# Sketch attention and a cosine router on one core: expert logits taken from the query product, four ticks per half, bfloat16 rank compares

## Chip, cores and metric

One core of one Trainium2 chip runs the whole program. The metric is device time in microseconds (us), the median of several executions; shorter is better.

## What is computed

Attention over 16 heads (batch 4, heads 4, sequence 1088, head size 32) with a polynomial feature map, then a router that sends each of 4352 tokens to one of 8 experts:

```python
a, b = S1 @ x, S2 @ x;  phi = outer(a, b)          # 8 x 8 = 64 features of q and of k
kv = sum_s phi(k)[s] v[s];  z = sum_s phi(k)[s]
x = (phi(q) @ kv) / (phi(q) @ z + 1e-6)             # heads side by side: 4352 x 128
xn = x / (|x| + 1e-6);  en = emb / (|emb| + 1e-6)
logits = xn @ en.T / tau;  e = argmax(logits)
out[token] = softmax(logits)[e] * (relu(x @ w1[e]) @ w2[e])
```

All data is float32.

## The kernel before

**Halves, tiles, groups.** The batch is worked in two halves m = 0, 1 (two batches each, 2176 tokens). A half has 17 tiles of 128 tokens, taken in the five groups of `GROUPS`: four of 4 tiles and a last one of 1 tile. Per group there are two helpers, `keys` (L296) and `queries` (L345), each a list of small functions:

- `keys`: `tr` transposes the tiles on TensorE (L267) and ScalarE copies them out (L269); `ab` forms both sketches (L280); `b` copies the second one (ScalarE, L286); `prod` multiplies them into 64 features (VectorE, L291, `kp`); `kv` adds the products with V into the PSUM bank `acc` (L327). After the last tile VectorE copies `acc` into `kz` (L335, L336).
- `queries`: `tr`, `ab`, `b`, `prod` as above (`qp`); `tr_qp` transposes the features (L372) and ScalarE copies them (L375, `qpT`); `nd` multiplies by `kz` (L383: 33 columns per head, value and denominator) and VectorE divides (L389 to L391, `xg`); `xt` transposes the result again (L397, copied by L399) and `logit` multiplies it by the normed experts `enT` (L412, copied by L415); `best` takes the maximum (L419); `squares` gives the norms (L404).
- `router`, every 8 tiles (`SPAN`): `pick` makes one-hot rows and counts (L452 to L462), `place` finds each token's slot (L471 to L482), `mark` compares 128 lane numbers with each token's rank (L487, `row`, one float32 operand), `store` finishes the norm (one GpSimd power, L493, and two VectorE operations), `write` stores `xg` to DRAM.

**Tables.** `plan_early` and `plan_late` turn counts into a list of 10 and of 31 expert blocks; `table` compares block keys with the slots (L541), multiplies by token digits (L545) and sums through TensorE (L550), one load of `row[:, t]` and one product per tile. The result lists which tokens each block gathers.

**Blocks.** 41 blocks of 128 tokens: `fetch` gathers rows (GpSimd, L605), `turn` transposes them (L611), `weights` copies an expert's weights (L623, L626 or L628), `up` is the first product (L637), `down` the second (L652), and GpSimd scatters the result (L657).

**What sets the order.** The order is written by hand: each function is put at a tick and a rank, and the program emits tick after tick, by rank within one. In the kernel before a group starts every second tick, and its steps spread over the ticks behind:

```python
put(0, 60, tr); put(1, 51, ab); put(1, 61, b); put(1, 63, prod); put(5 if late else 3, 30, kv)   # keys
put(0, 61, tr); put(1, 50, ab); put(1, 60, b); put(1, 62, prod)                                  # queries
put(3, 10, tr_qp); put(4, 20, nd); put(5, 20, xt); put(5, 80, squares); put(6, 10, logit); put(6, 70, best)
```

The keys of half 0 take ticks 0 to 9, the keys of half 1 with the queries of half 0 ticks 10 to 19, the queries of half 1 ticks 20 to 29, and the blocks start at tick 31. Each engine works in its own order and waits where an input is late. PSUM: two buffers `ps_t` for small results, two `ps_big`, and one bank each for `acc` and `ab`.

Of the kernel before, what the change touches and what calls it, by code (L numbers as in the profile page):

```python
# [13 lines left out]
I32 = mybir.dt.int32  # L14
# [19 lines left out]
GROUPS = ((0, 4), (4, 8), (8, 12), (12, 16), (16, 17))  # L34
SPAN = 8
ROW = DM + E + 1
DEN_EPS = 1e-6
# [16 lines left out]
def kernel(  # L54
# [47 lines left out]
    v_sb = [consts.tile([P, H + 1, NC, D], F32, name=f"v{m}") for m in range(NM)]  # L102
# [9 lines left out]
    def load_v(m, i):  # L112
        nc.sync.dma_start(
            v_sb[m][:, :H, i * NK:(i + 1) * NK].rearrange("p h c d -> p h (c d)"),
            bass.AP(tensor=v.tensor, offset=v.offset + (2 * m + i) * H * S * D,
                    ap=[[NK * D, P], [S * D, H], [1, NK * D]]))

    def load_rest(m):
        for i in range(2):
            r = slice(i * HALF, (i + 1) * HALF)  # L120
            at = (2 * m + i) * H * S * D + SK * D
            for t, src in ((k_rest[m][r], k), (v_sb[m][r, :H, NC - 1], v)):
                nc.sync.dma_start(t, bass.AP(tensor=src.tensor, offset=src.offset + at,
                                             ap=[[D, HALF], [S * D, H], [1, D]]))

    k_sb, q_sb = [None] * NM, [None] * NM
    emb_sb = consts.tile([E, DM], F32, name="emb_sb")
    tau_sb = consts.tile([E, 1], F32, name="tau_sb")
    for m in range(NM):
        k_sb[m] = rows_p.tile([P, H, 2, NK, D], F32, tag="rows", name=f"k{m}")  # L130
        for i in range(2):
            load_k(m, i)
            load_v(m, i)
        load_rest(m)
        q_sb[m] = rows_p.tile([P, H, NC, D], F32, tag="rows", name=f"q{m}")
        load_q(m)
        if m == 0:
            nc.sync.dma_start(emb_sb[:], emb)
            nc.sync.dma_start(tau_sb[:], bass.AP(tensor=tau.tensor, offset=tau.offset, ap=[[0, E], [1, 1]]))
# [9 lines left out]
    for m in range(NM):  # L149
        nc.gpsimd.memset(v_sb[m][:, H], 1.0)  # L150
# [38 lines left out]
    nc.gpsimd.memset(half_c, 0.5)  # L189

    rows = [tc.dram_tile([n, ROW], F32, name=f"rows{n}") for n in (2 * S, N)]

    def iota(shape, pattern, base, mult, name):
        ti = work.tile(shape, I32, tag="iota", name=name + "_i")
# [15 lines left out]
    lane_b = consts.tile([P, P], BF16, name="lane_b")  # L210
    nc.vector.tensor_copy(lane_b, lane)
    tok_i = consts.tile([P, 3, NT], I32, name="tok_i")
    nc.gpsimd.iota(tok_i[:, 0].rearrange("p (m c) -> p m c", m=NM), pattern=[[2 * S, NM], [1, NC]], base=1,
# [3 lines left out]
    digits = consts.tile([P, 2, NT], F32, name="digits")  # L217
# [6 lines left out]
    for w in (2, SPAN + 1):  # L224
# [11 lines left out]
    enT = consts.tile([P, E], F32, name="enT")  # L236
    kz = [consts.tile([P, 2, 2, 2, D + 1], F32, name=f"kz{m}") for m in range(NM)]
# [3 lines left out]
    def prep_emb():  # L241
        sq = work.tile([E, DM], F32, tag="emb", name="emb_sq")
# [53 lines left out]
    def keys(m, c0, c1, put, late):  # L296
# [6 lines left out]
        def ab(ps):  # L303
            s["ab"] = sketch(ps[:, 256:], s["kT"], n)
# [7 lines left out]
        def kv():  # L312
# [3 lines left out]

            end = ps_small()[:, :4 * D].rearrange("p (a n) -> p a n", a=2) if c1 == NC else None
            for c in range(c0, c1):
                rest = c == NC - 1
                for i in range(2) if rest else (c // NK,):  # L320
                    r = slice(i * HALF, (i + 1) * HALF) if rest else slice(0, P)
                    for p in range(2):
                        for u in range(2):
                            h = 2 * p + u
                            vo = v_sb[m][r, h, c]
                            own = acc[m][:, i] if not rest or i == 0 else end
                            nc.tensor.matmul(  # L327
                                own[u * HALF:(u + 1) * HALF, p], s["kp"][r, c - c0, h],
                                bass.AP(tensor=vo.tensor, offset=vo.offset,
                                        ap=[list(vo.ap[0]), [(H - h) * NC * D, 2], [1, D]]),  # L330
                                start=p == 0 and (c == 0 or own is end), stop=rest, skip_group_check=True)
            if c1 == NC:
                for u in range(2):
                    r = slice(u * HALF, (u + 1) * HALF)
                    nc.vector.tensor_copy(kz[m][r, :, :, u], acc[m][r, :, :, :D + 1])  # L335
                    nc.vector.tensor_add(kz[m][r, 1, :, u], kz[m][r, 1, :, u], end[r, :, :D + 1])  # L336
# [6 lines left out]
    xg, ssq = {}, {}  # L343

    def queries(m, c0, c1, put):  # L345
# [3 lines left out]
        g = (m, c0 // SPAN)  # L349
        at = c0 % SPAN  # L350
        own = slice(at, at + n)

        def tr():
            if at == 0:
                xg[g] = work.tile([P, SPAN, ROW], F32, tag="xg", bufs=3, name="xg")
                ssq[g] = work.tile([P, SPAN], F32, tag="ssq", name="ssq")
            s["qT"] = turned(None if n == 1 else q_sb[m][:, :, c0:c0 + 4], q_rest[m], n, "qT")

        def ab(ps):
            s["ab"] = sketch(ps[:, :256], s["qT"], n)  # L360
# [7 lines left out]
        def tr_qp():  # L368
            ps = ps_big()
# [4 lines left out]
            s["qpT"] = work.tile([P, 2, 512], F32, tag="qpT", name="qpT")  # L374
            nc.scalar.copy(s["qpT"][:, :, :w], ps[:, :, :w])  # L375

        def nd():
            ps = ps_big().rearrange("p b (u n) -> p (b u) n", u=2)
# [8 lines left out]
            hs = ps[:, :n, :2 * W].rearrange("p n (h d) -> p n h d", h=H)  # L387
            rc = work.tile([P, 4, H], F32, tag="rc", name="rc")
            nc.vector.tensor_scalar_add(rc[:, :n], hs[:, :, :, D], DEN_EPS)  # L389
            nc.vector.reciprocal(rc[:, :n], rc[:, :n])  # L390
            nc.vector.tensor_mul(xg[g][:, own, :DM].rearrange("p n (h d) -> p n h d", h=H), hs[:, :, :, :D],  # L391
                                 bview(rc[:, :n], [[H, n], [1, H], [0, D]]))

        def xt():
            ps = ps_small()
            for j in range(n):
                nc.tensor.transpose(ps[:, j * P:(j + 1) * P], xg[g][:, at + j, :DM], ident)  # L397
            s["xT"] = work.tile([P, 512], F32, tag="xT", name="xT")
            nc.scalar.copy(s["xT"][:, :w], ps[:, :w])  # L399

        def squares():
            for j in range(n):
                sq = work.tile([P, DM], F32, tag="sq", name="sq")
# [3 lines left out]
        def logit():  # L407
            ps = ps_small()[:, :4 * E].rearrange("p (n e) -> p n e", n=4)
            for j in range(n):
                for u in range(2):  # L410
                    r = slice(u * HALF, (u + 1) * HALF)
                    nc.tensor.matmul(ps[r, j], s["xT"][:, j * P + u * HALF:j * P + (u + 1) * HALF], enT,  # L412
                                     start=True, stop=True)
            s["lg"] = work.tile([P, 4, E], F32, tag="lg", name="lg")
            nc.scalar.copy(s["lg"][:, :n], ps[:, :n])  # L415

# [341 lines left out]
```

## Time and profile before

| what | us |
|---|---|
| time, median of 3 runs (283.9 to 286.25) | 285.73 |
| the profiled execution's own time | 285.32 |
| its span, first to last instruction | 283.5 |
| TensorE (PE) busy in it | 237.2 (84%) |
| VectorE (DVE) busy | 139.4 (49%) |
| ScalarE (ACT) busy | 117.9 (42%) |
| GpSimd (POOL) busy | 101.2 (36%) |

The profile is one execution. A matrix product in float32 stands in it as two records. A window row gives, for one stretch, the busy time of each engine and the granted TensorE clock as a share of 2.4 GHz (0.50 is 1.2 GHz). A timeline row gives start, length, engine, line, operation, tiles, count, and in brackets how long the engine stood idle before it and what ended that wait.

### The profile page before, as it was taken

The page shows a single profiled execution, that of the slowest core. Times are in us where ns is not written, and L with a number is a line of the kernel's source. Part 1 is how long each engine was busy: PE and PEld are TensorE (multiplying, and loading weights), DVE is VectorE, ACT ScalarE, POOL GpSimd, SP SyncE. Part 2 cuts the span into 40 slices and gives each one's busy share as a digit, 9 for nine tenths or more (in the row PEclk, how much of TensorE's full clock was granted, in tenths as well). Part 3 has the DMA queues.
Part 4 walks back from the last instruction along what each step waited for, and adds up shares of the span by engine and source line. Part 5 has one row for each costly group of instructions (what it writes and reads, how often), then busy time and mean ns, then how long its engine had stood idle before and what let it go on. Part 6 is the DMA issues. An engine that isn't in the chain of part 4 may idle for free. (4 is left out here: it accounts for less than half of the span.)

```text
span 283.5 us, 6567 instructions
## 1 busy us (share of the span) xinstructions
PE 237.2 (84%) x2558; PEld 226.7 (80%) x2558; DVE 139.4 (49%) x444; ACT 117.9 (42%) x315; POOL 101.2 (36%) x105
## 2 busy tenths in 40 slices
PE   1897788695939398597799999999999999999950
PEld 1786678694929288497799999999999999999950
DVE  6331445666872562437863455555544444444500
ACT  2222346435233344544564444444444444444420
POOL 4000000202000620715326765556666655554230
PEclk9995999959595856979999999999999999999995
DMA  5999999640300210111001211111011111121000
GB/s 197 258 314 205 318 341 338 190 161 16 145 20 2 86 46 0 48 64 48 19 21 34 48 41 30 41 33 41 27 35 38 39 38 34 33 37 30 18 0 0
DMA packets 22062, 24.32 MB, mean 86 GB/s; under 512 B 5321, under 2 KB 18004, under 8 KB 22032
## 3 DMA queue, kind: packets, MB, share of 16 engines
q1 hardware_dynamic: 19408, 18.79, 22.8%
q0 software_dynamic: 2624, 5.11, 7.0%
q8 instruction: 20, 0.33, 0.5%
q14 instruction: 10, 0.08, 0.1%
HBM read 18.09 MB, written 6.26 MB: 86 GB/s over the span
## 5 line engine op out<-in xcount | busy, mean ns | idle before, releaser
L637 PE MATMUL ps_big<-xTb,w1b 128*128 128x128 f32 x656 | 82.7, 281 | 1.9 <-DVE gate L645 1.9
L637 PEld LDWEIGHTS ps_big<-xTb,w1b 128*128 128x128 f32 x656 | 78.6, 196 | 2.6 <-DVE w1b L623 1.6
L638 ACT ACTIVATE hT<-ps_big 128x1024 f32<-128x1024 f32 x41 | 42.0, 1025 | 67.3 <-PE ps_big L637 67.2
L657 POOL DMA_INDIRECT out_dram<-y,dst_i x41 | 42.0, 1024 | 62.8 <-ACT y L654 59.5
L605 POOL DMA_INDIRECT xs<-rows,src_i x41 | 47.9, 1168 | 12.6 <-PE ps_t L611 7.8
L613 DVE COPY xTb<-ps_t 128x128 f32<-128x128 f32 x41 | 11.9, 291 | 59.8 <-PE ps_t L611 59.8
L652 PE MATMUL ps_acc<-w2b,hT 128*128 128x128 f32 x336 | 41.0, 275 | 0.0
L652 PE MATMUL ps_ab<-w2b,hT 128*128 128x128 f32 x320 | 40.0, 280 | 0.0
L652 PEld LDWEIGHTS ps_acc<-w2b,hT 128*128 128x128 f32 x336 | 39.2, 192 | 0.0
L652 PEld LDWEIGHTS ps_ab<-w2b,hT 128*128 128x128 f32 x320 | 38.5, 197 | 0.0
L493 POOL TENSOR_TENSOR xg<-ssq,half_c 128x8 f32<-128x8 f32 (+1 forms) x6 | 7.8, 1300 | 80.6 <-ACT lg L415 80.6
L623 DVE COPY w1b<-w_sb 128x1024 f32 x41 | 28.5, 696 | 9.0 <-issue 8.0
L628 DVE COPY w2b<-w_sb 128x1024 f32 x31 | 21.6, 698 | 0.0
L291 DVE TENSOR_TENSOR qp<-ps_ab,qb 128x1024 f32<-128x1024 f32 (+1 forms) x10 | 10.6, 1062 | 20.3 <-ACT kb L286 16.4
L611 PE MATMUL ps_t<-ident,xs 128*128 128x128 f32 x41 | 11.7, 285 | 4.9 <-DMA xs<-rows,src_i 4.9
L291 DVE TENSOR_TENSOR kp<-ps_ab,kb 128x1024 f32<-128x1024 f32 (+1 forms) x10 | 10.6, 1060 | 9.1 <-ACT kb L286 9.1
L383 PE MATMUL ps_big<-kz,qpT 128*64 128x66 f32 x272 | 14.7, 270 | 0.0
L375 ACT COPY qpT<-ps_big 128x1024 f32<-128x1024 f32 (+1 forms) x10 | 8.8, 885 | 12.6 <-PE ps_big L372 12.6
L383 PEld LDWEIGHTS ps_big<-kz,qpT 128*64 128x64 f32 x272 | 13.5, 178 | 0.0
L327 PE MATMUL ps_acc<-v,kp 128*64 128x64 f32 (+1 forms) x272 | 12.3, 255 | 1.2 <-DVE kz L336 1.2
L327 PEld LDWEIGHTS ps_acc<-v,kp 128*64 128x64 f32 (+1 forms) x272 | 10.8, 164 | 3.1 <-issue 2.6
L397 PE MATMUL ps_t<-ident,xg 128*128 128x128 f32 x34 | 7.2, 341 | 7.3 <-DVE mx L419 4.5
(162 smaller groups left out, 282.8 us busy)
## 6 DMA issues: line engine op xcount, KB each, us to landing
w_sb<-in_moe_w_dram SPq DMA_DIRECT2D x16, 512.0 KB, 7.9
rows<-xg SPq DMA_DIRECT2D x6, 548.0 KB, 2.9
q<-in_q_dram SPq DMA_DIRECT2D x4, 544.0 KB, 8.0
k<-in_k_dram SPq DMA_DIRECT2D x4, 512.0 KB, 5.8
v<-in_v_dram SPq DMA_DIRECT2D x4, 512.0 KB, 7.1
xs<-rows,src_i POOLq DMA_INDIRECT x41, 2.8
out_dram<-y,dst_i POOLq DMA_INDIRECT x41, 2.3
rows<-xg SPq DMA_DIRECT2D x3, 68.5 KB, 1.6
```

Source lines behind the costliest of these rows:

```text
L291: nc.vector.tensor_mul(t[:, :n].rearrange("p j h (i k) -> p (j h) i k", i=R), ab[:, :, 0].unsqueeze(3).broadcast_to([P, n * H, R, R]), b[: ...
L327: nc.tensor.matmul(own[u * HALF:(u + 1) * HALF, p], s["kp"][r, c - c0, h], bass.AP(tensor=vo.tensor, offset=vo.offset, ap=[list(vo.ap[0]), ...
L383: nc.tensor.matmul(ps[i * HALF:(i + 1) * HALF, j, p * W:(p + 1) * W], s["qpT"][:, p, j * P + i * HALF:j * P + (i + 1) * HALF], kz[m][:, i, ...
L605: nc.gpsimd.indirect_dma_start(out=xs[i][:], out_offset=None, in_=rows[t][:, :], in_offset=bass.IndirectOffsetOnAxis(ap=src_i[t][:, j:j + ...
L611: nc.tensor.transpose(ps[:, :P], xs[i][:, :DM], ident)
L613: nc.vector.tensor_copy(xT[i], ps[:, :P])
L623: nc.vector.tensor_copy(w1b[i], w1_sb[:, bass.ds(e, 1)].rearrange("p o f -> p (o f)"))
L628: nc.vector.tensor_copy(w2b[i], w2)
L637: nc.tensor.matmul(ps[:, u, j * P:(j + 1) * P], w[:, f * P:(f + 1) * P], x, start=True, stop=True)
L638: nc.scalar.activation(hT[i], ps, ACT.Relu)
L652: nc.tensor.matmul(ps, h[:, f * P:(f + 1) * P], w[:, f], start=f == 0, stop=f == NF - 1)
L657: nc.gpsimd.indirect_dma_start(out=out[:, :], out_offset=bass.IndirectOffsetOnAxis(ap=dst_i[t][:, j:j + 1], axis=0), in_=y[:], in_offset=N ...
```

## The change

Three parts.

**Logits from the query product.** While `kz` is made, the product of each head's K-V sum with the head's piece of the normed experts is formed once per half (`tr_kv`, `kvT`, `kve`: two small products and four ScalarE copies) and stored as 8 more columns per head. `nd` then gives 41 columns per head, and the logits are a scaled sum over the four heads on VectorE. `xt` and `logit` are gone, with their two ScalarE copies per group.

**Order.** The single tile 16 goes with the fourth group, so a half has four ticks, one per group: transposes, sketches, products at the group's tick, `kv`, `tr_qp`, `nd` and the division one tick later, router and squares two ticks later. Half 1's keys and half 0's queries stand at ticks 4 to 7, half 1's queries at 8 to 11, and the blocks start at tick 11. The last half tile of V has its own zero-padded tile `v_rest`, so its sums go into `acc` and the additions of L336 are gone. Spans are 8 and 9 tiles instead of 8, 8 and 1. `store` is three GpSimd operations (a second power takes the reciprocal's place).

**Rank compares.** `row` is stored with the tile as its last axis, and `mark` and `digit` have only bfloat16 operands. A load of one tile's `row` now reads every 36th element.

```diff
-GROUPS = ((0, 4), (4, 8), (8, 12), (12, 16), (16, 17))
+GROUPS = (((0, 4),), ((4, 8),), ((8, 12),), ((12, 16), (16, 17)))
...
+        def total():
+            s["kv"] = work.tile([P, 2, 2, D], F32, tag="kv", bufs=1, name="kv")
+            nc.scalar.copy(s["kv"], acc[m][:, :, :, :D])
...
+        def kve():
+            ps = ps_small()[:, :P // 2]
+            nc.tensor.matmul(ps, s["kvT"], en_blk.rearrange("p a u e -> p (a u e)"), start=True, stop=True)
...
-        put(0, 60, tr)
-        put(1, 51, ab)
-        put(1, 61, b)
-        put(1, 63, prod)
-        put(5 if late else 3, 30, kv)
+        put(0, 10, tr)
+        put(0, 50, ab)
+        put(0, 61, b)
+        put(0, 63, prod)
+        put(1, 30, kv)
...
-            W = 2 * (D + 1)
+            W = 2 * COLS
...
+            t = work.tile([P, 4, H, E], F32, tag="parts", bufs=1, name="parts")[:, :n]
+            nc.vector.tensor_mul(t, hs[:, :, :, D + 1:], bview(rc, [[H, n], [1, H], [0, E]]))
+            nc.vector.reduce_sum(out=lg[g][:, own], in_=t.rearrange("p n h e -> p n e h"), axis=AX.X)
...
+        put(0, 62, prod)
+        put(1, 20, tr_qp)
+        put(1, 70, nd)
+        put(1, 75, x)
+        put(2, 25, lambda: squares(0, 2))
+        put(2, 65, lambda: squares(2, 4))
...
-            nc.vector.tensor_tensor(out=row[:, t0:t1], in0=bview(lane_b, [[0, n], [1, P]]),
-                                    in1=place_f[:, 1, t0:t1].unsqueeze(2).broadcast_to([P, n, P]), op=ALU.is_equal)
+            nc.vector.tensor_tensor(out=row[:, :, t0:t1], in0=lanes[:, :, :w],
+                                    in1=bview(place_r[:, t0:t1], [[0, P], [1, w]]), op=ALU.is_equal)
...
+            nc.gpsimd.tensor_scalar(d, d, NORM_EPS, None, op0=ALU.add)
+            nc.gpsimd.tensor_tensor(out=d, in0=d, in1=minus_c[:, :n], op=ALU.pow)
...
+                nc.tensor.matmul(s["ps"].rearrange("p (d n) -> p d n", d=2), row[:, :, t], s["col"][:, :, :, t],
+                                 start=t == tiles[0], stop=t == tiles[-1])
```

TensorE in the middle of the keys of half 1 and the queries of half 0, one group. Before (`ps_t<-ident,xg` is `xt`, `enT,xT` is `logit`, `kz,qpT` is `nd`):

```order
L267 MATMUL ps_t<-ident,k_94 128x128 x4
L267 MATMUL ps_t<-ident,q_87 128x128 x4
L372 MATMUL ps_big<-ident,qp 128x128 x8
L397 MATMUL ps_t<-ident,xg 128x128 x4
L327 MATMUL ps_acc<-v_71,kp 64x64 x16
L280 MATMUL ps_ab<-Sblk,qT 64x4x16 x8
L280 MATMUL ps_ab<-Sblk,kT 64x4x16 x8
L412 MATMUL ps_t<-enT,xT 64x8 x8
L383 MATMUL ps_big<-kz_213,qpT 64x66 x16
```

The same group in the changed kernel:

```order
L290 MATMUL ps_t<-ident,k_106 128x128 x4
L290 MATMUL ps_t<-ident,q_101 128x128 x4
L426 MATMUL ps_big<-ident,qp 128x128 x8
L356 MATMUL ps_acc<-v_71,kp 64x64 x16
L306 MATMUL ps_ab<-Sblk,qT 64x4x16 x8
L306 MATMUL ps_ab<-Sblk,kT 64x4x16 x8
L437 MATMUL ps_big<-kz_226,qpT 64x82 x16
```

The two steps `xt` and `logit` are out of the row and `nd` is wider; `tr_qp` and `kv` now take the features of the group directly before, where they took those of an earlier group.

VectorE in the queries of half 1, from the end of the early plan (`c_early`, `took`) to the early table (`hit`, `col`, `lo`). Before:

```order
L574 TENSOR_SCALAR c_early<-upto_1130 128x8
L576 TENSOR_TENSOR took<-c_early 128x8
L291 TENSOR_TENSOR qp<-ps_ab,qb 128x1024
L487 TENSOR_TENSOR row<-lane_b,place_f 128x128
L541 TENSOR_TENSOR hit_225<-at_1138,place_f 128x170
L545 TENSOR_TENSOR col_226<-hit_225,digits 128x17x10 x2
L552 COPY lo_1192<-ps_t 128x10
```

Changed:

```order
L637 TENSOR_SCALAR c_early<-upto_244 128x8
L639 TENSOR_TENSOR took<-c_early 128x8
L537 TENSOR_TENSOR row<-lanes,place_r 128x128x10
L595 TENSOR_TENSOR hit_1064<-at_1052,place_k 128x180
L599 TENSOR_TENSOR col_1065<-hit_1064,digits 128x180 x2
L611 COPY lo_1123<-ps_t 128x10
```

The group's feature product `qp` no longer stands between plan and table, and the compare `row` there is one of a whole span of 9 tiles (10 columns), where a single tile's stood.

TensorE from the first `turn` (`ident,xs`) to the first `up` (`xTb,w1b`). Before, the first `up` is the row behind these:

```order
L611 MATMUL ps_t<-ident,xs 128x128
L372 MATMUL ps_big<-ident,qp 128x128 x8
L397 MATMUL ps_t<-ident,xg 128x128 x4
L471 LDWEIGHTS before
L471 MATMUL ps_t<-oh,before 128x64
L472 LDWEIGHTS ones
L472 MATMUL ps_t<-cum,ones 128x64
L277 MATMUL ps_ab<-Sblk,qT 64x64 x2
L412 MATMUL ps_t<-enT,xT 64x8 x8
L383 MATMUL ps_big<-kz_214,qpT 64x66 x16
L372 MATMUL ps_big<-ident,qp 128x128 x2
L397 MATMUL ps_t<-ident,xg 128x128 x4
```

Changed:

```order
L680 MATMUL ps_t<-ident,xs 128x128
L437 MATMUL ps_big<-kz_227,qpT 64x82 x16
L515 LDWEIGHTS before
L515 MATMUL ps_t<-oh,before 128x64
L516 LDWEIGHTS ones
L516 MATMUL ps_t<-cum,ones 128x64
L706 MATMUL ps_big<-xTb,w1b 128x128 x8
```

One `nd` and one `place` are left between the two; the fourth group's `tr_qp`, which stood there before, now follows the first `up`.

## Rows read from the trace of the kernel before

**Rows 1.** Windows: us, busy us (x instructions) by engine, granted clock, DMA share, GB/s

```profile
0.00:23.40 23.40, 13.94 (x183) 11.79 (x183) 10.73 (x49) 5.44 (x13) 3.47 (x17) 0.98 0.96 255
23.40:61.60 38.20, 32.04 (x570) 29.12 (x570) 18.69 (x42) 16.47 (x54) 1.68 (x1) 0.86 0.94 275
61.60:107.50 45.90, 32.37 (x389) 28.68 (x388) 27.96 (x104) 17.17 (x61) 8.82 (x8) 0.72 0.14 49
107.50:141.10 33.60, 26.77 (x218) 25.30 (x217) 17.93 (x73) 16.50 (x42) 12.16 (x11) 0.89 0.12 38
141.10:271.20 130.10, 130.10 (x1190) 129.98 (x1190) 63.88 (x176) 61.56 (x144) 73.08 (x66) 1.00 0.13 34
271.20:283.50 12.30, 1.98 (x18) 1.78 (x16) 0.16 (x1) 0.73 (x2) 1.95 (x2) 0.66 0.00 0
```

**Rows 2.** Timeline of TensorE, one group of keys and queries

```profile
37.40 0.66 PE L267 MATMUL ps_t<-ident,k 128*128 128x128 f32 x4
37.90 0.60 PE L267 MATMUL ps_t<-ident,q 128*128 128x128 f32 x4
38.34 1.10 PE L372 MATMUL ps_big<-ident,qp 128*128 128x128 f32 x8
40.65 0.63 PE L397 MATMUL ps_t<-ident,xg 128*128 128x128 f32 x4 [1.22 <-DVE xg L391]
41.21 1.15 PE L327 MATMUL ps_acc<-v,kp 128*64 128x64 f32 x32
42.19 0.74 PE L280 MATMUL ps_ab<-Sblk,qT 128*64 128x64 f32 x13
...
43.92 1.16 PE L383 MATMUL ps_big<-kz,qpT 128*64 128x66 f32 x30
45.02 0.66 PE L267 MATMUL ps_t<-ident,k 128*128 128x128 f32 x4
```

**Rows 3.** Timeline of TensorE: long waits, and one product at either clock

```profile
55.87 0.63 PE L397 MATMUL ps_t<-ident,xg 128*128 128x128 f32 x4 [2.08 <-DVE mx L419]
...
59.60 2.06 PE L383 MATMUL ps_big<-kz,qpT 128*64 128x66 f32 x32
...
83.98 0.62 PE L550 MATMUL ps_t<-col,row 128*128 128x20 bf16 x17 [3.81 <-DVE col L545]
...
92.30 1.19 PE L383 MATMUL ps_big<-kz,qpT 128*64 128x66 f32 x32
...
98.68 0.45 PE L611 MATMUL ps_t<-ident,xs 128*128 128x128 f32 x1 [4.94 <-DMA xs<-rows,src_i]
```

**Rows 4.** Waits: who waited for whom, us in total, times, longest

```profile
PE ps_t L253 <- DVE emb_sq L251: 2.2, 1, 2.2
```

**Rows 5.** Groups by line and shape: busy us, mean ns of one, idle before

```profile
L291 DVE TENSOR_TENSOR qp<-ps_ab,qb 128x1024 f32<-128x1024 f32 x8 | 9.8, 1224 | 20.3 <-ACT kb L286 16.4 <-ACT qb L286 3.9
...
L375 ACT COPY qpT<-ps_big 128x1024 f32<-128x1024 f32 x8 | 8.1, 1012 | 10.3 <-PE ps_big L372 10.3
...
L493 POOL TENSOR_TENSOR xg<-ssq,half_c 128x8 f32<-128x8 f32 x4 | 6.7, 1665 | 75.4 <-ACT lg L415 75.4
...
L487 DVE TENSOR_TENSOR row<-lane_b,place_f 128x1024 bf16<-128x1024 bf16 x4 | 4.8, 1210 | 0.0
...
L550 PE MATMUL ps_t<-col,row 128*128 128x62 bf16 x34 | 1.2, 192 | 0.0
...
L454 DVE TENSOR_REDUCE mx<-lt 128x8 f32<-128x64 f32 x4 | 0.9, 220 | 0.1
...
L391 DVE TENSOR_TENSOR xg<-ps_big,rc 128x128 f32<-128x128 f32 x2 | 0.6, 292 | 0.1
```

**Rows 6.** Timeline of VectorE: first and last of the early plan's operations

```profile
79.51 0.17 DVE L566 TENSOR_SCALAR n_early<-n_early 128x8 int32<-128x8 int32 x1
...
81.56 0.17 DVE L576 TENSOR_TENSOR took<-c_early 128x8 f32<-128x8 f32 x1
```

**Rows 7.** DMA issues: KB each, median us from issue to landing

```profile
xs<-rows,src_i POOLq DMA_INDIRECT x41, 2.8
```

More of the change, by code (lines that the diff above doesn't have):

```diff
@@ L394, in xt @@
[L394 to L403, printed above, removed]
+            s["hs"] = ps[:, :n, :2 * W].rearrange("p n (h d) -> p n h d", h=H)
@@ L404, in squares @@
+        def squares(j0, j1):
+            for j in range(j0, min(j1, n)):
+                sq = work.tile([P, DM], F32, tag="sq", bufs=1, name="sq")
                 nc.scalar.activation(sq, xg[g][:, at + j, :DM], ACT.Square,
                                      accum_out=ssq[g][:, at + j:at + j + 1])
[L407 to L415, printed above, removed]
@@ L575, in plan_early, with count, rest @@
-        early["took"] = column("took")
-        nc.vector.tensor_sub(early["took"], c_early[:, 1:], c_early[:, :E])
+        def count():
+            ps = ps_small()[:, :E]
+            nc.tensor.matmul(ps, ones, counts[0], start=True, stop=True)
+            nc.vector.tensor_sub(ni, ps, region)
+        def rest():
+            nc.vector.tensor_scalar(ni, ni, 7, None, op0=ALU.logical_shift_right)
+            nc.vector.tensor_copy(full, ni)
+            nc.vector.tensor_tensor_scan(out=upto[:], data0=ones[:, :E], data1=full[:], initial=0.0, op0=ALU.mult, op1=ALU.add)
+            nc.vector.tensor_scalar(w, full, -1.0, float(KEYS), op0=ALU.mult, op1=ALU.add)
+            at = blocks(0, upto, w)
+            nc.vector.tensor_add(at, at, lane[:, :EARLY])
+            early["key"] = at
+            nc.vector.tensor_scalar_min(c_early[:, 1:], upto, float(EARLY))
+            early["took"] = column("took")
+            nc.vector.tensor_sub(early["took"], c_early[:, 1:], c_early[:, :E])
@@ L594, in plan_late, with count, rest @@
-        late["key"] = at
+        def count():
+            ps = ps_small()[:, :E]
+            nc.tensor.matmul(ps, ones, counts[0], start=True, stop=True)
+            nc.vector.scalar_tensor_tensor(out=ni, in0=ps, scalar=float(P - 1), in1=region, op0=ALU.add, op1=ALU.subtract)
+        def rest():
+            took = early["took"]
+            nc.vector.tensor_scalar(ni, ni, 7, None, op0=ALU.logical_shift_right)
+            nc.vector.tensor_copy(all_, ni)
+            nc.vector.tensor_sub(left, all_, took)
+            nc.vector.tensor_tensor_scan(out=upto[:], data0=ones[:, :E], data1=left[:], initial=0.0, op0=ALU.mult, op1=ALU.add)
+            nc.vector.tensor_sub(t[:, :E - 1], took[:, 1:], all_[:, :E - 1])
+            nc.vector.tensor_scalar_add(w_late[:, :E - 1], t[:, :E - 1], float(KEYS))
+            at = blocks(1, upto, w_late)
+            nc.vector.scalar_tensor_tensor(out=at, in0=at, scalar=took[:, 0:1], in1=lane[:, :LATE], op0=ALU.add, op1=ALU.add)
+            late["key"] = at
@@ L661, in first_block @@
     def first_block():
-        for i in range(AHEAD):
-            fetch(i)
         weights(0)
```

359 lines of the change are left out of this document (190 added, 169 removed).

## Prediction

> **What bounds the kernel now.** I read first the windows [rows 1], which cut the span where the work changes: keys of half 0 to 23.4 us; keys of half 1 with queries of half 0 to 61.6; queries of half 1 to the first expert product at 107.5; six expert blocks mixed with the last of the queries to 141.1; 35 blocks to 271.2; the end. In the fifth stretch TensorE is busy 130.1 of 130.1 us at full clock. Nothing of the change is done there but the late table's sums, so it is a fixed cost of 130.1 / 35 = 3.7 us a block. In the three stretches before it TensorE is idle 6.2, 13.5 and 6.8 us, and the granted clock is 0.86, 0.72 and 0.89: time is lost to waits and to half clock. Then I read TensorE's timeline through one group [rows 2]: 7.6 us from 37.40 to 45.02, of which one wait is 1.22, for the division before `xt`. The long waits [rows 3] show the second cost: behind a wait of 2.08 us the product of `nd` takes 2.06 us where it takes 1.19 elsewhere, and the waits of 3.81 (early table) and 4.94 (gathered rows) stand in the stretch with the lowest clock. So before 141 us the kernel is bound by chains between the engines, and each wait over about 2 us is paid again by a stretch at 1.2 GHz. VectorE (28.0 of 45.9) and ScalarE (17.2) are not full there.
>
> The sum is made stretch by stretch against the profiled execution, 285.32 us: span 283.5 and 1.8 around it. The median of the runs is 0.4 above. A difference of about 1% is what measuring this kernel can tell from none.
>
> **Keys of half 0, 23.4 us before.** The fifth round goes, and with it the experts' transpose that TensorE waited 2.2 us for [rows 4]. Added is a wait in each tick: `kv` now stands one tick behind its product, so from the sketch's end TensorE waits for the copy and the 1.22 us product [rows 5] with only one group's transposes beside it; about 1 us in each of three ticks, some of it hidden by the loads. Queued behind that `kv` is the next sketch, for which the whole loop waits. Between no gain and 4 us less I take 1.9 less: 21.5.
>
> **Keys of half 1, queries of half 0, 38.2 us before.** From the starts in [rows 2] a group costs TensorE 0.50 + 0.44 for transposes, about 0.9 for `tr_qp` (the spacing of transposes, 0.11, times 8), 0.56 for `xt`, 0.98 for `kv`, and 45.02 - 42.19 = 2.83 for sketches, `logit` and `nd`: 6.2 of its 7.6. Without `xt` and `logit` (about 0.5) it is 5.15. `nd` has 82 columns for 66. Its 32 records take 1.19, so the cost is between nothing and 24%, 0.3 us; I take 0.15, as loading the weights does not grow. That is 5.3 a tick. Is a one-tick lag hidden? Behind the end of the query sketch stand 0.55 of key sketch, 1.3 of `nd` and 0.94 of transposes, 2.8 us, while the product needs 0.3 + 1.22; the key product follows 1.2 later and `kv` 0.9 later: hidden, with 0.5 to spare. The 1.01 us copy of `qpT` has `kv` and sketches, 2 us, beside it. VectorE gains two operations a group, a product out of PSUM of 128 elements (0.29 by the row of that shape) and a sum of 128 elements (0.22 at 64, at most double), 0.6 in all, and loses the additions of `kz`: near 4 us of the tick, not the bound. ScalarE loses two copies. The experts' columns of `kz` add five small steps between `kv` and the first `nd`: a wait of about 0.7 in tick 5. The first tick waits about 1.6 for the products of tile 16, whose sketches hold a `ps_t` buffer; the last carries tile 16 and waits 1.2 on the same buffer. Ticks of 6.2, 5.6, 5.4 and 7.8: 25.0.
>
> **Queries of half 1 to the first `up`, 45.9 us before.** Tick 8: 5.6 us of work with half 1's last `kv`, then 2.5 idle until VectorE has divided two `nd` and freed a `ps_t` buffer: 8.3. That wait halves the clock: tick 9 has 3.4 us of work and takes 7.4. Then VectorE is the bound. From this group's product to the early table's last digit it works through 1.2 (product), 0.5, 1.7 (division and logits), 1.0 (slots), the plan's 2.1 from 79.51 to 81.6 [rows 6], one compare, and 0.9 for hit and digits: 8 in a row. TensorE reaches the early sums early and waits about 4.5, as it waited 3.81 before. So tick 10 is 10.4. In tick 11 the first gather needs 0.9 for tokens, 1.2 to issue and 2.8 to land [rows 7] behind the sums; `nd`, transposes, `tr_qp` and sketches, 6 us at half clock, cover it, so the 4.94 us wait goes. What is late next is `place`, 2 us behind VectorE's products. 8.1. Sum 34.2, the first `up` at 80.7 instead of 107.5. The weights are in SBUF by then: DMA traffic falls from 275 GB/s to 49 after 61.6 in [rows 1].
>
> Compares: `mark` has 1024 elements and 1.21 us with a float32 operand. No row has a compare or product with bfloat16 operands alone: between 1.21 (no gain) and half its time, 0.6. I take 0.65, since the operand kept from 16 bits is what the change removes; at 1.21 the sum rises by 1.3 for all compares and digits. The Trainium skill ("VectorE: DVE Perf Modes", "The perf-mode tier table") has two-operand operations at two elements a cycle when all is 16 bits wide, and one for float32; by its figures a compare would be an estimated 0.69, which moves the sum by nothing.
>
> Three GpSimd operations stand for one: 1.67 [rows 5] becomes at most 3 x 1.8 = 5.4, at least 2 x 1.7. Behind them queue the first gathers; by the sum they start some 6 us after the last store of half 0 ends, so this is covered. Without that cover it would cost 2 to 4 us once.
>
> **Loads of `row`.** 34 records of the late sums take 1.2 us, 35 ns each, with `row[:, t]` contiguous; 17 belong to the early ones. Every 36th element may cost nothing or bring a pair to the 110 ns that a 128-wide float32 record takes in the full stretch (130.1 / 1190): 51 x 75 ns = 3.8. I take 1.6. The Trainium skill ("SBUF — State Buffer", "Specifications (TRN2)") speaks against this part: SBUF is read in 16-byte lines and wants two hits in each, and here every element is in a line of its own. It names no price; by the upper bound the sum would be 2.2 us more.
>
> **Six blocks with the last queries, 33.6 us before.** Six blocks are 22.1 of TensorE; `tr_qp`, `nd`, `place` of what is left 3.2 and the late sums 1.2, which leave the next stretch. VectorE has plan, table and a compare in the blocks' way: two waits of 2 us, and two stretches at half clock, 5 us. With 35.4 I take 1.8 more than before.
>
> **Sum.** 21.5 + 25.0 + 34.2 + 35.4 + (130.1 - 1.2) + 12.3 + 1.8 = 259.1. The same adding of durations along the engines' orders, done for the kernel before, ends 2.8 us short of its trace; I add them, and 1.6 for `row`: 263.5, and 0.4 to the median: 263.9.
>
> **Rivals.**
> - *The waits stay short.* If VectorE is done sooner in ticks 8 to 11, no wait passes 2 us and the clock stays up: the three slow stretches assumed here go, 10 us: 254. For it: waits of 1.2 us in [rows 2] left the clock alone. Against it: the early table's wait was 3.81 and its chain is no shorter.
> - *Half clock from tick 8 to the full stretch.* If a wait over 2 us comes in each tick and each early block, the 28 us of work that I count there at full clock double; some 10 of that would go into waits that stand there anyway, and 18 are added: 282. For it: 0.72 in that stretch of [rows 1], and a one-tick lag leaves less room than the old spread.
> - *Slower: the lag itself.* If copies and products do not fit beside TensorE's work, every tick from 4 to 11 waits over 2 us and runs at half clock. Their 37 us of work at full clock become 74, with 8 x 2.3 of waits 92 instead of 59.2: 297. It decides from 3 us more per tick on (24 over eight). Against it: 5.3 us of work against some 4 us on VectorE, and 2.8 us of cover for a 1.5 us chain.
> - *The compares gain nothing.* 1.3 us, and with the upper bound of `row` 3.5: 267.4, within my own range.
>
> **Chances.** Forecast with the last rival 0.66 (own range 256 to 272), short waits 0.17, half clock throughout 0.12, slower 0.05. Range 250 to 279: it holds the first two and the near part of the third. Faster by over 1%: 0.66 + 0.17 + 0.10 = 0.93; slower 0.04; between 0.03.
>
> **What would show it.** Right: the first `up` between 78 and 88 us, the full stretch unchanged at 3.7 us a block, TensorE's longest wait before it at the early sums, on a digit product of VectorE. The compare row near 0.65 us says that the bfloat16 part works; `row` loads over 110 ns a pair break that bound. Wrong: waits over 2 us in ticks 4 to 7 (the lag), a wait of `turn` on gathered rows, or a first `up` after 100.

## Result and the profile after

The changed kernel takes 259.77 us (median of 4 runs, 259.00 to 260.12) beside 285.85 for the kernel before in the same job: a ratio of 0.9096, 95% interval 0.9050 to 0.9143. The forecast was 263.9 and faster. The profiled execution has a span of 257.2 us and 1.8 around it. The kernel before scatters more than the changed one: the 283.90 to 286.25 of this job, and the profiled 285.32, are mostly slower executions of a kind that the ratios of the later jobs leave out, and beside faster ones (280.51 to 283.74) the same changed kernel has a ratio of 0.9201 (e9), a gain of 8% instead of 9. The experiments below are given with their median as well as with their ratio.

First the windows, cut where the same work begins and ends as in [rows 1], with the same columns:

```profile
0.00:22.20 22.20, 12.97 (x184) 11.33 (x184) 10.84 (x53) 4.89 (x11) 4.75 (x26) 1.00 0.93 248
22.20:48.50 26.30, 22.18 (x442) 20.08 (x439) 17.24 (x33) 13.85 (x45) 2.11 (x3) 1.00 1.08 301
48.50:77.40 28.90, 22.74 (x327) 20.36 (x328) 22.44 (x83) 14.51 (x48) 9.47 (x8) 0.88 0.47 158
77.40:115.70 38.30, 31.68 (x271) 30.46 (x272) 23.27 (x80) 20.43 (x56) 19.59 (x17) 0.91 0.16 53
115.70:244.70 129.00, 129.00 (x1155) 128.80 (x1153) 61.23 (x172) 60.62 (x142) 70.76 (x65) 1.00 0.14 33
244.70:257.20 12.50, 2.19 (x20) 1.99 (x18) 0.32 (x2) 0.74 (x3) 1.96 (x2) 0.72 0.00 0
```

| stretch | before | predicted | after |
|---|---|---|---|
| keys of half 0 | 23.4 | 21.5 | 22.2 |
| keys of half 1, queries of half 0 | 38.2 | 25.0 | 26.3 |
| to the first `up` | 45.9 | 34.2 | 28.9 |
| six blocks, late sums with them in the last column | 33.6 | 35.4 | 38.3 |
| 35 blocks | 130.1 | 128.9 | 129.0 |
| end | 12.3 | 12.3 | 12.5 |

28.9 us are gone between 22 us and the first `up`, 4.7 came back in the six blocks behind it. The reader sees why in the timeline of TensorE: one tick of keys and queries as in [rows 2] (33.82 to 39.26, 5.44 us without a wait), then the long waits that are left, the sums and the `up` products behind them.

```profile
33.82 0.66 PE L290 MATMUL ps_t<-ident,k 128*128 128x128 f32 x4
34.31 0.60 PE L290 MATMUL ps_t<-ident,q 128*128 128x128 f32 x4
34.75 1.04 PE L426 MATMUL ps_big<-ident,qp 128*128 128x128 f32 x8
35.71 1.15 PE L356 MATMUL ps_acc<-v,kp 128*64 128x64 f32 x32
36.70 0.74 PE L306 MATMUL ps_ab<-Sblk,qT 128*64 128x64 f32 x13
...
37.99 1.34 PE L437 MATMUL ps_big<-kz,qpT 128*64 128x82 f32 x30
39.26 0.66 PE L290 MATMUL ps_t<-ident,k 128*128 128x128 f32 x4
...
48.57 0.92 PE L290 MATMUL ps_t<-ident,q 128*128 128x128 f32 x4 [2.39 <-issue]
...
68.53 1.21 PE L605 MATMUL ps_t<-col,row 128*128 128x20 bf16 x17 [3.85 <-DVE col L599]
69.67 2.51 PE L437 MATMUL ps_big<-kz,qpT 128*64 128x82 f32 x32
...
77.49 2.02 PE L706 MATMUL ps_big<-xTb,w1b 128*128 128x128 f32 x16
83.66 3.78 PE L706 MATMUL ps_big<-xTb,w1b 128*128 128x128 f32 x16 [1.72 <-DVE gate L714]
92.05 2.05 PE L706 MATMUL ps_big<-xTb,w1b 128*128 128x128 f32 x16
...
104.30 2.02 PE L706 MATMUL ps_big<-xTb,w1b 128*128 128x128 f32 x16 [2.18 <-DVE gate L714]
...
111.74 4.24 PE L605 MATMUL ps_t<-col,row 128*128 128x62 bf16 x34
115.79 1.97 PE L706 MATMUL ps_big<-xTb,w1b 128*128 128x128 f32 x16
```

Where `up` waits for `gate`, it waits for the copy of `w1b`: it does not read `gate`, and the copy is what VectorE does right ahead of it. The profile names nothing for the wait of 2.39 us, but its cause can be found. The two `ps_t` buffers are used in turn, and the transposes that wait need the one that holds the sketches of tile 16 until VectorE has made the last product of that tick. That product ends at 48.36, and the transposes start at 48.57; in e1 below the two stand at 49.56 and 49.78.

```profile
47.95 0.41 DVE L317 TENSOR_TENSOR kp<-ps_t,kb 128x256 f32<-128x256 f32 x1
```

The 34 pairs of the late sums take 4.24 us, where [rows 5] had 1.2. The groups by line and shape show the other side of that edit: a mark (L537), the digits (L599), and the two new operations of the logits (L452, L453).

```profile
L453 DVE TENSOR_REDUCE lg<-parts 128x32 f32<-128x128 f32 x8 | 3.0, 380 | 0.3
L452 DVE TENSOR_TENSOR parts<-ps_big,rc 128x128 f32<-128x128 f32 x8 | 2.2, 280 | 0.0
L599 DVE TENSOR_TENSOR col<-hit,digits 128x1116 bf16<-128x1116 bf16 x2 | 1.5, 731 | 0.1
L537 DVE TENSOR_TENSOR row<-lanes,place_r 128x1024 bf16<-128x1024 bf16 x2 | 1.4, 709 | 0.1
```

### The profile page after: what moved, and what is told of

Same layout as the page of the kernel before. It is cut to its first block, busy times and chain, and to the rows that moved or that the text cites. A ratio compares the mean times of both kernels' runs of the same rounds, so it can differ in the third digit from the quotient of the medians.

```text
span 257.2 us, 6199 instructions
## 1 busy us (share of the span) xinstructions
PE 220.7 (86%) x2391; PEld 213.0 (83%) x2391; DVE 135.3 (53%) x421; ACT 115.0 (45%) x303; POOL 108.6 (42%) x120
## 5 line engine op out<-in xcount | busy, mean ns | idle before, releaser
L721 PEld LDWEIGHTS ps_acc<-w2b,hT 128*128 128x128 f32 x336 | 40.4, 197 | 0.0
L721 PEld LDWEIGHTS ps_ab<-w2b,hT 128*128 128x128 f32 x320 | 37.3, 192 | 0.0
L697 DVE COPY w2b<-w_sb 128x1024 f32 x31 | 21.5, 693 | 0.0
L317 DVE TENSOR_TENSOR kp<-ps_ab,kb 128x1024 f32<-128x1024 f32 x8 | 9.8, 1219 | 9.0 <-ACT kb L312 9.0
L437 PE MATMUL ps_big<-kz,qpT 128*64 128x82 f32 x256 | 13.0, 251 | 0.7 <-issue 0.6
L317 DVE TENSOR_TENSOR qp<-ps_ab,qb 128x1024 f32<-128x1024 f32 x8 | 9.8, 1224 | 7.1 <-ACT kb L312 6.2
L437 PEld LDWEIGHTS ps_big<-kz,qpT 128*64 128x64 f32 x256 | 11.5, 147 | 1.4 <-issue 0.8
L723 ACT ACTIVATE y<-ps_acc,gate 128x128 f32<-128x128 f32 x21 | 7.7, 368 | 10.6 <-PE ps_acc L721 10.6
L458 ACT ACTIVATE sq<-xg 128x128 f32<-128x128 f32 x34 | 10.6, 312 | 3.1 <-DVE rc L447 2.2
L711 ACT ACTIVATE probs<-xs 128x8 f32<-128x8 f32 x41 | 11.9, 291 | 0.0
L356 PEld LDWEIGHTS ps_acc<-v,kp 128*64 128x64 f32 x256 | 9.2, 152 | 3.1 <-DVE kp L317 1.1
```

The lines of the kernel that those rows point to most:

```text
L317: nc.vector.tensor_mul(t.rearrange("p j h (i k) -> p (j h) i k", i=R), ab[:, :, 0].unsqueeze(3).broadcast_to([P, n * H, R, R]), b.unsqueez ...
L437: nc.tensor.matmul(ps[i * HALF:(i + 1) * HALF, j, p * W:(p + 1) * W], s["qpT"][:, p, j * P + i * HALF:j * P + (i + 1) * HALF], kz[m][:, i, ...
L697: nc.vector.tensor_copy(w2b[i], w2)
L711: nc.scalar.activation(p, xs[i][:, DM:DM + E], ACT.Exp, scale=xs[i][:, ROW - 1:], accum_out=gate[i])
L721: nc.tensor.matmul(ps, h[:, f * P:(f + 1) * P], w[:, f], start=f == 0, stop=f == NF - 1)
```

## The experiments

### Which strided operand makes the sums dear (e1, e2, e3)

The layouts were undone one at a time: `col` alone, `row` alone, both.

```diff
-                s["col"] = work.tile([P, 2, n, w], BF16, tag="xg", bufs=3, name="col1")
...
+                s["col"] = work.tile([P, w, 2, n], BF16, tag="xg", bufs=3, name="col1")
...
-    row = consts.tile([P, P, NM * NCP], BF16, name="row")
+    row = consts.tile([P, NM * NCP, P], BF16, name="row")
```

e1 has the first edit (with `hit` and the early table alike), e2 the second; e3 has both, with `place_r` and `digits` in float32 and no padding column in the marks.

Expected of e1:

> Only the layout of the table's digits (`col`, and `hit` with it) goes back to one contiguous row per tile; `row` keeps its strided columns. Theory A, the strided moving operand costs: the 34 late pairs fall from 4.24 us to 1.2 to 1.6, the 17 early ones from 1.21 to about 0.6, digits and hits take about 1.24 us again for 0.73, and since the late sums stand on the path to the full stretch the time falls by about 2 us, to 257 or 258. Theory B, the strided weights cost: the late pairs stay near 4 us, the digits still get dearer, and the time is the same or 1 us longer.

Expected of e2:

> Only the rank marks (`row`) go back to one contiguous row of 128 per tile, written with broadcast operands; `col` stays strided. Theory A, the moving operand costs: late pairs stay near 4 us, a mark takes about 1.2 us for 0.71 to 0.82, time 260 to 261. Theory B, the weights cost: late pairs fall to 1.2 to 1.6 us and the weight load of such a pair from 152 ns to about 100; time 257 to 258.

Expected of e3:

> The whole part on rank compares is undone: marks and digits contiguous per tile, float32 operands in them as before. If the faster compares lie beside TensorE's work and the strided sums on the path, as the trace suggests, the time falls by 2 to 3 us against the changed kernel (256.5 to 258). If the compares carried the gain, marks of 1.2 us and hits and digits of 1.24 put 1 to 3 us back on the path, and the time is 261 to 264.

Measured: e1 255.82 us (ratio 0.9012, 0.8962 to 0.9062), e2 262.02 (0.9204, 0.9138 to 0.9270), e3 257.28 (0.8994, 0.8904 to 0.9085). Groups of the sums, the marks and the digits, e1 first, then e2, then e3:

```profile
L599 DVE TENSOR_TENSOR col<-hit,digits 128x1116 bf16<-128x1116 bf16 x2 | 2.6, 1314 | 0.1
L605 PE MATMUL ps_t<-col,row 128*128 128x62 bf16 x34 | 2.2, 222 | 0.0
```

```profile
L605 PE MATMUL ps_t<-col,row 128*128 128x62 bf16 x34 | 4.2, 301 | 0.0
L537 DVE TENSOR_TENSOR row<-lanes,place_r 128x1024 bf16<-128x1024 bf16 x2 | 2.5, 1225 | 0.1
...
L605 PE MATMUL ps_t<-col,row 128*128 128x20 bf16 x17 | 0.8, 208 | 4.5 <-DVE col L599 4.5
```

```profile
L537 DVE TENSOR_TENSOR row<-lanes,place_r 128x1024 bf16<-128x1024 bf16 x2 | 2.5, 1226 | 0.1
...
L605 PE MATMUL ps_t<-col,row 128*128 128x62 bf16 x34 | 1.2, 192 | 0.0
```

Busy time over pairs gives 4.24 / 34 = 125 ns with both strided, 2.17 / 34 = 64 with strided weights alone (e1), 125 again with a strided moving operand alone (e2), 35 with neither (e3). So `col`, the moving operand, carries the late sums (theory A), and the weights have a price of their own that it hides: with both strided the pair takes the larger of the two, not their sum. The early pairs, with 20 columns, confirm it: 1.21 / 17 = 71 ns in the changed kernel, 69 with strided weights alone, 49 with a strided `col` alone. Theory A had the late pairs of e1 at 1.2 to 1.6 us; the 64 ns of the weights were not in it.

The compares themselves gain 0.5 us each and lie beside TensorE's work: undoing all of this part (e3) costs nothing and gives 1% by the medians. The gain of e1 is clear: its runs (253.72 to 257.16) lie below every run of the changed kernel (258.98 to 260.41). In e1 the seventh `up` starts at 110.40, 5.4 us earlier than in the changed kernel; 2.0 of them are the sums, and 2.9 the second block (83.66 to 92.05 in the changed kernel, 82.96 to 88.47 in e1), which ran at half clock in the one profile and not in the other.

### Does the wait at the early sums cost its half clock (e4)

```diff
+FILL = (34, 0)
...
-            s["ps"] = ps_small()[:, :2 * n]
+            full = ps_small()
+            s["ps"] = full[:, :2 * n]
+            for _ in range(FILL[which]):
+                nc.tensor.transpose(full[:, 128:256], ident, ident)
```

Expected of e4:

> 34 extra transposes of a constant, 0.11 us each, are put on TensorE ahead of the early table's sums, where it waits 3.85 us; nothing reads them. Theory C, the wait brings the half clock: the granted clock stays at 1.00 behind the sums, the product of `nd` there takes 1.25 us and not 2.51, and the first `up` comes 1 to 2 us earlier, of which part reaches the end (258 to 259.5). Rival: the clock falls all the same, or the gathered rows set the first `up`; then it stays at 77.5 and the time at 260.

Measured: 259.05 us (0.9101, 0.9033 to 0.9169), the same as the changed kernel. The clock does what theory C says: in the timeline the fill takes the place of the wait and `nd` behind it takes 1.41 us.

```profile
64.41 3.93 PE L606 MATMUL ps_t<-ident 128*128 128x128 f32 x34
68.33 1.17 PE L609 MATMUL ps_t<-col,row 128*128 128x20 bf16 x17
69.43 1.41 PE L438 MATMUL ps_big<-kz,qpT 128*64 128x82 f32 x32
...
76.99 2.02 PE L710 MATMUL ps_big<-xTb,w1b 128*128 128x128 f32 x16
```

`nd` and the transposes behind it take 1.4 us less, and the first `up` comes 0.5 us earlier, no more. The windows of that stretch say why, changed kernel first, then e4: from 73 to 77 us TensorE now has less to do (2.92 of 4.00 for 3.56), and VectorE is as busy as before (3.15 of 4.00). Its copy of `xTb`, which the first `up` reads, comes only 0.5 us earlier, and in both the product starts 0.12 us behind it.

```profile
70.00:73.00 3.00, 3.00 (x38) 2.82 (x35) 2.42 (x8) 0.00 (x0) 2.04 (x2) 0.56 0.09 23
73.00:77.00 4.00, 3.56 (x58) 3.00 (x57) 3.15 (x11) 2.96 (x8) 2.02 (x3) 1.00 0.24 53
...
77.09 0.28 DVE L682 COPY xTb<-ps_t 128x128 f32<-128x128 f32 x1
```

```profile
70.00:73.00 3.00, 2.95 (x44) 2.45 (x41) 2.72 (x8) 1.03 (x3) 2.17 (x2) 1.00 0.09 23
73.00:77.00 4.00, 2.92 (x53) 2.39 (x51) 3.15 (x12) 3.24 (x11) 1.90 (x2) 1.00 0.23 57
...
76.59 0.28 DVE L686 COPY xTb<-ps_t 128x128 f32<-128x128 f32 x1
```

So here most of the half clock was paid out of time in which TensorE would have waited for VectorE anyway.

### Order or logits (e5, e6)

e5 keeps the new order and makes the logits in the old way; e6 puts the new logits into the old order.

```diff
+        put(2, 55, xt)
+        put(2, 76, logit)
...
-            put(1, 80, best)
...
+            put(2, 80, best)
...
-    for plan, which, m1, after in ((plan_early, 0, 1, 1), (plan_late, 1, NM, 5)):
+    for plan, which, m1, after in ((plan_early, 0, 1, 2), (plan_late, 1, NM, 6)):
```

That is e5, with `COLS = D + 1` and without `parts`, `tr_kv`, `kvT` and `kve`; `pick` moves with `best`, and `store` to `write` one tick. e6, an edit of the kernel before:

```diff
-        put(5, 20, xt)
         put(5, 80, squares)
-        put(6, 10, logit)
-        put(6, 70, best)
+        put(5, 70, best)
...
-    put_at(tick)(5, 50, plan_early)
+    put_at(tick)(4, 50, plan_early)
```

with `place` to `write`, tables, late plan and blocks one half tick earlier, and the new preparation of the experts.

Expected of e5:

> The new order, the bfloat16 compares and the four groups stay; the logits are made in the old way again: `xg` transposed a tick after its division, multiplied with the experts, and everything behind it (ranks, plans, blocks) one tick later; the experts' columns of `kz` and the small steps that make them are out. Theory D, the order carries most of the gain: eight groups get about 0.8 us of TensorE more, one tick of 5 to 8 us stands ahead of the first expert block, and 264 to 272 us come out, so that more than half of the 26 us stays. Theory E, the logits carry it: the chain from `nd` to the ranks is the bound again, TensorE waits over 2 us a tick, and the time is 275 or more.

Expected of e6:

> The kernel before, in its old order of two ticks a group and with a round of its own for tile 16, with the new logits alone: the experts' columns in `kz`, `nd` of 82 columns, no `xt`, no `logit`, and ranks, plans and blocks one (half) tick earlier. Theory D, the order carries most of the gain: a group saves 0.5 to 0.8 us of TensorE and the end of each chain about 2 us, so 274 to 281. Theory E, the logits carry it: 265 to 270, and the first `up` below 90 us.

Measured: e5 262.73 us (0.9306, 0.9209 to 0.9402), e6 280.52 (0.9944, 0.9901 to 0.9988). The windows of e5 from the first transposes of half 1's queries alone to the first `up` and on to the seventh; then those of e6 for the second and third stretch, cut as in [rows 1]:

```profile
47.26:85.28 38.02, 29.91 (x483) 26.54 (x483) 26.66 (x93) 21.03 (x71) 16.61 (x14) 0.91 0.39 136
85.28:119.94 34.66, 29.44 (x248) 27.94 (x245) 18.75 (x66) 17.65 (x44) 14.80 (x13) 0.95 0.15 50
```

```profile
23.40:61.66 38.26, 30.92 (x513) 28.13 (x514) 21.36 (x55) 15.10 (x52) 1.68 (x1) 0.83 0.93 273
61.66:104.15 42.49, 25.31 (x301) 21.47 (x299) 29.29 (x111) 14.82 (x56) 9.81 (x9) 0.73 0.16 54
```

Theory D holds, and e5 came out even below the 264 us that it gave. In the old order the new logits take 7 us of busy time off TensorE in the third stretch (25.31 for 32.37 in [rows 1]), and the stretch is only 3.4 us shorter: idle time takes most of what was saved, at a granted clock of 0.73 as before. The new order with the old logits keeps most of the gain: its first `up` comes 7.8 us behind the changed kernel's, its seventh 4.1, its end 3. By its ratio the order with the compares is worth 19.6 us without the new logits ((1 - 0.9306) x 282.1, the mean that the ratio is formed with). By the ratio of e6 the new logits are worth 1.6 us in the old order; in the new one they are worth 3.0 by the medians. There the ratio of e5 stands clear of the changed kernel's first interval (0.9050 to 0.9143) and overlaps that of its second job below, so the 3 us are no firm number.

### One tick per group, or the merged last group (e10, e12)

```diff
-GROUPS = (((0, 4),), ((4, 8),), ((8, 12),), ((12, 16), (16, 17)))
+GROUPS = (((0, 4),), ((4, 8),), ((8, 12),), ((12, 16),), ((16, 17),))
```

In e10 the late plan stands one tick ahead of the last group's ranks, so it counts without them and the output is not the kernel's; e12, which puts it one tick later, behind them, and the late sums ahead of the block of their tick, is the one that decides.

Expected of e10:

> The changed kernel with one thing undone: tile 16 has a group and so a tick of its own in each of the three rounds; one tick per group, the new logits and the compares stay. If the merged last group carries much of the order's gain, three ticks come back, each with its chain of transposes, copy, sketch, copy and product of a single tile on the path (2.5 to 4 us): 7 to 12 us more than the changed kernel. If the shorter lag alone carries it, under 4 us more.

Expected of e12:

> As the one before with a tick of its own for tile 16 in each round, but with the late plan one tick later, behind the last group's ranks, and the late sums ahead of the seventh block. If the merged last group carries part of the order's gain, the time is 3 us or more above the changed kernel (ratio over 0.925); if the one-tick lag alone carries it, it stays within 2 us of it (0.91 to 0.925).

Measured: e10 258.71 us (0.9165, 0.9093 to 0.9238), e12 257.58 (0.9134, 0.9067 to 0.9202). The changed kernel ran again beside e10 (e9), and gave 259.72 us (0.9201, 0.9124 to 0.9277); its ratio missed what was expected, for the reason given with the result. Expected of e9:

> The changed kernel itself, for a time on the same chip as the two beside it: every theory expects its ratio again, 0.905 to 0.915.

A tick of its own for tile 16 costs nothing. It even takes away the wait of 2.39 us: the transposes of half 1's first queries, the first row here, start without one. The sums and the first `up` of e12 come 1.6 us earlier than the changed kernel's 68.53 and 77.49:

```profile
50.64 0.66 PE L290 MATMUL ps_t<-ident,q 128*128 128x128 f32 x4
...
66.86 1.21 PE L605 MATMUL ps_t<-col,row 128*128 128x20 bf16 x17 [3.88 <-DVE col L599]
75.87 2.05 PE L706 MATMUL ps_big<-xTb,w1b 128*128 128x128 f32 x16
```

What is left of the order is one tick per group with its new ranks, and by elimination that carries the gain; e5, with one tick more ahead of its first `up`, has it 7.8 us later. The smaller edits that e5 keeps (the experts loaded earlier, `v_rest` with zeros) were not tried apart, nor the ranks within a tick.

### Moving VectorE's work out of TensorE's way (e7, e8, e11)

All three have the contiguous digits of e1. e7 moves three pieces of VectorE's work, e8 adds 16 transposes ahead of the early sums, e11 moves more.

```diff
-        put(1, 75, x)
+        put(1, 89 if (m, c0) == (1, 0) else 75, x)
...
-            put(2, 84, mark)
+            put(2 + g[0] * g[1], 90 if m else 84, mark)
...
-            put(after + 3, 56, sums)
...
+            put(after + 4, 53, sums)
```

These are the edits of e7, with `high` and `low` of the late table a tick later. e11 has besides the transposes of e8: `best` to `split` and the mark of half 1's first span one tick later, the late plan in two ticks, the mark of the second span three ticks later.

Expected of e7:

> The changed kernel with contiguous digits as in the first experiment, and VectorE's work in another order: the division of half 1's first group stands behind the early table, the marks of half 1 behind the expert block of their tick, and the late table is spread over one tick more, with its sums ahead of the seventh block instead of behind the sixth. If VectorE's order sets TensorE's waits from the early sums to the seventh block, the wait at the early sums falls from 4.0 to about 2.3 us, those ahead of the second and fifth block below 1 us, and the time to 249 to 253. Rival: the waits only move to another block, or the clock falls elsewhere; then 254 to 257, as the first experiment.

Expected of e8:

> The same with 16 extra transposes of a constant ahead of the early sums. If what is left of the wait there still halves the clock, these bring the product of `nd` behind it from 2.5 to 1.3 us and 1 us at the end against the kernel without them; if the shorter wait leaves the clock alone, both are the same within 0.5 us.

Expected of e11:

> Contiguous digits, the 16 extra transposes, and VectorE's work moved once more: ranks and slots of half 1's first group behind the first expert blocks, the late plan in two pieces and its mark last. If VectorE's order is what sets the first `up` and the waits of the early blocks, the first `up` comes at 75 to 76 us, the waits ahead of the second and fifth block go below 1 us, up to the seventh `up` 3 to 5 us go, and the ratio is 0.875 to 0.89. Rival: from 60 to 83 us VectorE is full, and what is moved only comes back later; then 0.893 to 0.90, as with the two before.

Measured: e7 254.05 us (0.8999, 0.8894 to 0.9103), e8 252.68 (0.8959, 0.8885 to 0.9034), e11 254.55 (0.9018, 0.8947 to 0.9088). All three are faster than both kernels: their runs (252.23 to 254.76) lie below every run of the changed one. By the medians e8 gains 7 us or 2.7% over it, and its interval lies clear of both intervals of the changed kernel (0.9050 and 0.9124 upward); by their intervals they are not told apart among themselves and from e1. In e8 `nd` behind the early sums takes 1.42 us for 2.51 in e7, as expected. The rest went as the rivals had it. In e7 the first wait fell as expected, those ahead of the second and fifth block did not go below 1 us, and one ahead of the late sums is new:

```profile
67.95 1.18 PE L605 MATMUL ps_t<-col,row 128*128 128x20 bf16 x17 [2.46 <-DVE col L599]
...
83.28 2.05 PE L706 MATMUL ps_big<-xTb,w1b 128*128 128x128 f32 x16 [1.79 <-DVE gate L714]
...
99.74 2.02 PE L706 MATMUL ps_big<-xTb,w1b 128*128 128x128 f32 x16 [1.57 <-DVE gate L714]
...
108.51 2.19 PE L605 MATMUL ps_t<-col,row 128*128 128x62 bf16 x34 [1.16 <-DVE col L599]
```

In e11 the first `up` comes at 76.21 and the second at 80.65, 3 us ahead of the changed kernel's; then the ranks that were put off are late for the plan, and the fourth `up` waits and runs at half clock:

```profile
93.20 0.17 PE L653 MATMUL ps_t<-cum,ones 128*128 128x8 bf16 x1 [2.50 <-DVE cum L508]
95.00 0.20 PE L517 MATMUL ps_t<-oh,before 128*128 128x72 bf16 x1 [1.62 <-DVE xTb L690]
...
95.60 3.46 PE L714 MATMUL ps_big<-xTb,w1b 128*128 128x128 f32 x16 [0.37 <-DVE gate L722]
```

e8 has the granted clock at 1.00 in both of its windows and still TensorE is idle 3.6 of 17.5 and 5.6 of 32.5 us in them, with VectorE at 15.4 and 24.4:

```profile
60.00:77.50 17.50, 13.88 (x213) 12.32 (x212) 15.41 (x59) 10.45 (x36) 8.00 (x7) 1.00 0.24 89
77.50:110.00 32.50, 26.94 (x272) 25.56 (x271) 24.44 (x80) 19.45 (x51) 20.38 (x17) 1.00 0.18 62
```

## Why the prediction was right, step by step

- **What bounds the kernel** held: the chains ahead of the full stretch were the cost, and the full stretch stayed at 129.0 / 35 = 3.69 us a block.
- **Keys of half 0**: 22.2 for 21.5. The removed wait of 2.2 us for the experts' transpose came back whole, as two waits (1.74 and 0.72 us) that the profile puts down to `emb` and `emb_ss`, the new preparation of the experts.
- **Keys of half 1, queries of half 0**: 26.3 for 25.0. By the starts of their first transposes, ticks 4 to 7 took 5.9, 5.7, 5.4 and 9.3 us, for 6.2, 5.6, 5.4 and 7.8. The error is in tick 7: the wait for tile 16's products was priced at 1.2 and is the 2.39 us one. That is a wait over 2 us, one of the prediction's signs of being wrong, but e12 puts it down to the merged last group and not to the lag. The lag of one tick is hidden: no other wait in these ticks is over 0.73 us. `nd` grew by 16% (30 records 1.34 us for 1.16), 0.18 for the 0.15 assumed. The rival of the lag falls with this.
- **To the first `up`**: 28.9 for 34.2. Ticks 8 to 11 took 8.4, 5.3, 9.9 and 5.4 us, for 8.3, 7.4, 10.4 and 8.1. Tick 8 is right by luck: the 2.5 us of idle time behind two divisions did not come (0.52 is there), and a granted clock of 0.80 took its place. The wait at the early sums was 3.85 us on a digit product (4.5 assumed), and `turn` no longer waits for gathered rows. What was too large was the half clock: tick 9 and tick 11 were charged some 4 and 3 us for it, and ran at 1.00 and 0.95; in the trace the clock is 0.88 over the whole stretch (0.12 x 28.9 = 3.5 us of work), and e4 shows that removing the half clock behind the early sums gives 0.5. The first `up` came at 77.5, half a microsecond ahead of the 78 to 88 stated as a sign.
- **Waits and half clock.** That each wait over about 2 us is paid again at 1.2 GHz does not hold. The wait of 2.39 us is followed by transposes of 1.91 us in the changed kernel and of 1.04 in e1. The `up` behind 2.18 us took 2.02 us, full clock, and the one behind 1.72 took 3.78.
- **Compares**: 709 ns for 1024 elements, 650 assumed, against 1210 in [rows 5]. The Trainium skill ("VectorE: DVE Perf Modes", "The perf-mode tier table") gave an estimated 0.69 us; the trace agrees with it better than with my 0.65. That the layout has a part in it was not foreseen (last section).
- **Loads of `row`**, the step that failed. It charged 1.6 us for strided weights, at most 3.8, with no price for `col` as the moving operand. Measured: (4.24 - 1.2) + (1.21 - 0.6) = 3.65 us, within the 3.8, but e1 and e2 put the late part on `col`. The upper bound of 110 ns a pair was passed (125). The Trainium skill ("SBUF — State Buffer", "Specifications (TRN2)") spoke against this part and was right in sign.
- **Six blocks**: 38.3 for 35.4. Two waits on VectorE were foreseen and came (1.72 and 2.18 us), one stretch at half clock came where two were assumed; the late sums at 4.24 us instead of 1.2 are the 3 us that were missing (1.6 of them stood in the sum under `row`).
- **The sum** met the time by offset: 5.3 us too much in one stretch, 4.9 too little in three others. The 2.8 us added because the same adding came out short for the kernel before had no counterpart in the trace.
- **Rivals**: that the waits stay short came half true, since the waits came and their half clock cost little. e3 shows that the compares gain nothing at the end, although each of them is faster, because they lie beside TensorE's work.

## What to carry to other kernels

When operands are laid out anew for a faster engine, price the one that reads them next: here VectorE won 0.5 us an operation beside the path and TensorE lost 3.65 us on its sums. A stretch that is made of chains was shortened here, by elimination, by fewer ticks between two ends of a chain more than by the work that one step loses: the logits were worth 1.6 to 3 us, the order with the compares nearly 20. And half clock need not cost its full price: in e4 1.4 us of it came to 0.5, since VectorE was what the next step waited for. Look at what the other engines do behind it before charging it.

## What the runs showed of the hardware

- A strided moving bfloat16 operand (a step of 36 elements in the late table, 18 in the early one) costs TensorE about (125 - 49) / (62 - 20) = 1.8 ns a column; weights at a step of 36 make a pair of 35 ns one of 64; both together the larger of the two. The Trainium skill ("SBUF — State Buffer", "Who interferes with whom") gives TensorE two independent read ports for the moving operand and the weights, and these rows agree.
- A compare of two bfloat16 operands is no faster than one with a float32 operand when one of them is broadcast along the innermost axis: 1225 ns for 1024 elements in e2, with everything in bfloat16 and `place_r` broadcast, 1226 with the float32 operand of e3, against 709 with `lanes` and `place_r` laid out along the tiles. The prediction gave the whole gain to the type. The Trainium skill ("Vector Engine (DVE) Microarchitecture Reference", "Performance modes — why throughput varies by op and dtype") has one element read again and again as a source of such an operation at 1x, and the rows agree.
- Two profiled executions of the changed kernel show half clock in different places (the second, fourth and seventh `up` at 3.78, 2.05 and 1.97 us in the one, 3.38, 2.99 and 3.33 in the other), at times of 259.00 and 260.10. So a single product at half clock in one profile is no proof of what an edit did.
- Behind the late sums with a strided `col` the next `up` ran wholly or in part at half clock in three of seven profiles (e2, e4, e9: 3.02, 3.54 and 3.33 us), behind the contiguous ones in none of six. That the slow stream brings it was not tested by itself.
